# Where the moving operands of the first layer's products start: 32 bytes further into tiles that all start at multiples of 64 bytes

## The chip, the cores and the metric

The kernel runs on one core of one Trainium2 chip. The metric is the device time of one execution in microseconds; it is given as the median of several runs of the same program, and one further execution was taken with the hardware profiler.

## What is computed

Linear attention with an RMS norm per head, then a two-layer network with a GELU between its layers. The reference, cut to what matters:

```python
# q, k, v: (8, 8, 576, 64); g_norm: (64,); w_in: (512, 2048); w_out: (2048, 512)
kv = np.einsum('bhsd,bhse->bhde', k, v)
out = np.einsum('bhsd,bhde->bhse', q, kv)
rms = np.sqrt(np.mean(out * out, axis=-1, keepdims=True) + 1e-06)
out = out / rms * g_norm
x = out.transpose(0, 2, 1, 3).reshape(4608, 512)
h = x @ w_in
g = 0.5 * h * (1.0 + erf(h / sqrt(2)))
return g @ w_out
```

## The kernel before, in words

The 4608 tokens are cut into nine chunks of 512. Every operand of the two big layers is held as two float32r parts, a high and a low one, and a product takes three matmuls: high by high, low by high, high by low. Weights and activations stand in a pool named `const`, mostly in tiles of 128 partitions by 4096 bytes (`w_in0` to `w_in15`, `w_out0` to `w_out15`, `x0` to `x5`), which are used again for other things once their first content has been read.

Chunks 0 and 1 run the first layer plainly (`layer1`, L508 to L524): per block of 128 hidden units twelve matmuls of 512 columns, weights stationary, activations moving. While chunk 1 runs, the weights are summed and differenced into the seven operands of Strassen's scheme in Winograd's form and written to memory (`combine`, `high_sums`, `low_sums`, `product_out`).

Chunks 2 to 8 run the first layer by that scheme (`layer1_pair`, L412 to L450). Two hidden blocks form a pair j. It has seven products, and each is six matmuls (L427): the stationary operand is a 128 by 128 piece of one of four ring tiles, the moving one is 256 columns of one of seven pieces of the chunk's activations:

```python
    def product(k, out, first=False):
        n = ((at.c - PLAIN) * NF // 2 + j) * NPR + k
        w, x = ring[n // 2][:, n % 2 * DM:(n % 2 + 1) * DM], at.x[k]
        for kb in range(2):
            hi, lo = (w[:, m * HALF + kb * P:m * HALF + (kb + 1) * P] for m in range(2))
            for i, (y, z) in enumerate(((hi, 0), (lo, 0), (hi, 1))):
                nc.tensor.matmul(out=out, lhsT=y, rhs=x[:, z, kb], ...)
```

The ring tiles (`w_in0` to `w_in3`) are loaded again from memory as soon as their two products are done (`load_products`, L407 to L410). The seven pieces of a chunk stand in `x2`, `x3`, `w_in5` to `w_in9` for even chunks and in `x0`, `x1`, `x4`, `x5`, `w_in10` to `w_in12` for odd ones (`piece_tile`, L343 to L346). ScalarE writes a piece's high half (`high_block`, L317), GpSimd or VectorE its low half (`low_block`, L323), while the chunk before runs. Between the products VectorE adds their results in PSUM (L419, L437).

The second layer (`layer2`, L541 to L549) takes 24 matmuls of 512 columns per pair (L546): the GELU's results are stationary, the rows of `w_out` move. A chunk's eight pairs follow one another (L934 to L947): seven products, then the second layer of the pair before, with the next chunk's projections (`project`, L196 to L209, 64 to 512 columns of `qh` and `ql`, or of `w_in4`, moving against `kv_h` and `kv_l`) put between in the pairs 0 to 2.

The order on every engine is the order of the program (a manual schedule). The tensor engine's weight loads (PEld) run beside its matmuls (PE).

The program also has a tile `warm` of zeros (L78), on which 28 dummy matmuls run in the first 19 us (`keep_warm`, L596).

Of the kernel before, what the change touches and what calls it, by code (L numbers as in the profile page):

```python
# [8 lines left out]
F32 = mybir.dt.float32  # L9
F32R = mybir.dt.float32r  # L10
I32 = mybir.dt.int32
# [5 lines left out]
P = 128  # L17
EPS = 1e-6
CH = 512
# [3 lines left out]
HALF = CH // 2  # L23
# [12 lines left out]
def linear_attn_rms_gelu_ffn(  # L36
# [18 lines left out]
    NT, DM = out.shape  # L55
    B, NP = kv_main.shape[:2]
# [4 lines left out]
    NF = w_in.shape[0]  # L61
# [4 lines left out]
    const = ctx.enter_context(tc.tile_pool(name="const", bufs=1))  # L66
# [8 lines left out]
    kv_l = [const.tile([P, NP, P], F32R, name=f"kv_l{s}") for s in range(2)]  # L75
    ident = const.tile([P, P], F32, name="ident")
    fold = const.tile([P, P], F32, name="fold")
    warm = const.tile([P, P], F32, name="warm")  # L78
    half_g = const.tile([P, 1], F32, name="half_g")
    heads = const.tile([P, 2], F32, name="heads")  # L80


    kv_in, late = {}, {}

    def late_tile(name):

        if name not in late:
            late[name] = const.tile([P, 2 * DM], I32, name=name).bitcast(F32)
        return late[name]

    def load_main(b, p):
# [16 lines left out]
    def load_kv(b, p):  # L108

        early = b == 0 or (b == 1 and p > 1)  # L110
        if early:
            main = late_tile(f"w_out{NF - 1 - p if b == 0 else NF - 3 - p}")
        else:
            main = work.tile([P, 2 * DM], I32, name="kv_main", bufs=2).bitcast(F32)
        nc.sync.dma_start(out=main, in_=kv_main[b, p])
        main = main.rearrange("p (a n) -> p a n", a=2)[:KROWS]
        if b == 0:
            tails = late_tile(f"w_in{NF - 1}")[:TAIL].rearrange("p (a n) -> p a n", a=NP)
            if p == 0:
                nc.sync.dma_start(out=tails, in_=kv_tail[0])  # L120
            tail = tails[:, p]
        else:
            if early:
                tail = late_tile(f"w_in{NF - 5}")[:, (p - 2) * 2 * P:(p - 1) * 2 * P]
            else:
                tail = work.tile([P, 2 * P], I32, name="kv_tail", bufs=2).bitcast(F32)
            tail = tail[:TAIL]
            nc.sync.dma_start(out=tail, in_=kv_tail[b, :, p])
        tail = tail.rearrange("p (a n) -> p a n", a=2)
        parts = [main[:, :, j * P:(j + 1) * P] for j in range(NJ)] + [tail]  # L130
        kv_in[b, p] = [(t[:, 0], t[:, 1]) for t in parts]
# [29 lines left out]
    class Attn:  # L161
# [119 lines left out]
            self.low_x(p, eng)  # L281

        def high_x(self, p):
            x = const.tile([P, 2, CH], F32R, name=f"x{(NP * self.c + p) % 6}")
            nc.scalar.copy(out=x[:, 0], in_=self.o[p])
            self.x[p] = x

# [29 lines left out]
        def high_block(self, n):  # L317

            x = piece_tile(self.c, n)
            nc.scalar.copy(out=x[:, 0], in_=self.block(OPERANDS[n]))  # L320
            self.x[n] = x
# [13 lines left out]
    kept = {}  # L335

    def reused(i, dtype=F32):

        if i not in kept:
            kept[i] = const.tile([P, 2 * DM], dtype, name=f"w_in{i}")  # L340
        return kept[i]

    def piece_tile(c, n):  # L343
        k = (["x2", "x3"] + [f"w_in{i}" for i in range(5, 10)],
             ["x0", "x1", "x4", "x5"] + [f"w_in{i}" for i in range(10, 13)])[c % 2][n]
        return const.tile([P, 2, 2, HALF], F32R, name=k)  # L346

    products = [dram.tile([P, 2 * DM], F32, name=f"products{t}") for t in range(NT2)]

# [35 lines left out]
    def high_sums():  # L385

        for (j, second), s in stage.items():
            if j % 2:
                t = reused(second, F32R).rearrange("p (k a n) -> p k a n", k=2, a=2)
            else:  # L390
                t = const.tile([P, 2, 2, HALF], F32R, name=f"x{2 + second}")
            nc.scalar.copy(out=t[:, :, 0], in_=s)
            halved[j, second] = s, t
        stage.clear()
# [12 lines left out]
    def load_products(t):  # L407
        if t < (NCH - PLAIN) * NT2:
            ring[t] = reused(t % RING, F32R)
            nc.sync.dma_start(out=ring[t].bitcast(F32), in_=products[t % NT2])  # L410

    def layer1_pair(at, j, between):  # L412


        a, b = (ps_h.tile([P, CH], F32, name="ps_h") for _ in range(2))
        left, right = slice(0, HALF), slice(HALF, CH)
        u = reused(15).rearrange("p (a n) -> p a n", n=HALF)
        p1, u2, v, u3 = (u[:, i] for i in range(4))
        add = lambda out, x, y: nc.vector.tensor_tensor(out=out, in0=x, in1=y, op=ALU.add)  # L419
# [38 lines left out]
    raw, parts = {}, {}  # L458

    def load_w(n):  # L460
        kind, i = weights[n]
        src = w_in[i] if kind == "in" else w_out[i * P:(i + 1) * P, :]
        raw[n] = const.tile([P, 2 * DM], I32, name=f"w_{kind}{i}")
        nc.sync.dma_start(out=raw[n], in_=src.bitcast(I32))

    zs, ws = {}, {}
# [27 lines left out]

    def high_w(n):
        kind, i = weights[n]
        t = const.tile([P, 2 * DM], F32R, name=f"w_{kind}{i}")
        parts[kind, i] = t
        nc.scalar.copy(out=t[:, HI], in_=ws[n].bitcast(F32))

# [59 lines left out]

    attn = [Attn(c) for c in range(NCH)]
    first, second = attn[:2]
    nc.vector.memset(warm, 0.0)
    nc.scalar.activation(out=heads, in_=warm[:, :2], func=AF.Gelu)
    mask, g_row = late_tile(f"w_in{NF - 6}")[:, :P], late_tile(f"w_in{NF - 6}")[:1, P:2 * P]
# [11 lines left out]
    for h in range(2):  # L577
        nc.scalar.dma_start(out=g_row[:, h * D:(h + 1) * D], in_=g_norm.unsqueeze(0))
    load_w(0)
    for p in range(2):  # L580
        load_kv(1, p)
    for n in (1, 2, 3):
        load_w(n)
    for p in (2, 3):
        load_kv(1, p)
    load_w(4)
    second.load(0)
    for n in range(5, 9):
# [47 lines left out]
    n = 2 * NB  # L636
# [45 lines left out]
    for p in (2, 3):  # L682
        bcs[p] = ps_acc.tile([P, DM], F32, name=f"acc{p}")
        for t in range(NG):
            for h, r in enumerate((slice(0, D), slice(D, 2 * D))):
                k = n + 2 * ((p - 2) * NG + t) + h
# [82 lines left out]
    def sum_weights(i, n, gelu_rest):  # L769

        high_sums()
        for k in range(n):
            if k:
                high_sums()
            combine(*halves.pop(0))
            if not k:
                gelu_rest()
            low_sums()
        if not n:
            gelu_rest()  # L780
            low_sums()
# [22 lines left out]
    def convert(i, gelu_rest, between):  # L804

        count = 3 if i in (2, 4, 6, 8) else 2 if i < 11 else i in (11, 12, 14)
        now = [order.pop(0) for _ in range(count)]
        for k, n in enumerate(now or [None]):  # L810
            if last:
                high_w(last[0])
                if last[0] + 2 < len(weights):
                    top_w(last[0] + 2)
            if not i and not k:
                gelu_rest()
                low_w(last.pop())
            if n is not None:
                bits_w(n)
            if i and not k:  # L820
                gelu_rest()
            if last:
                low_w(last.pop())
            if n is not None:
                last.append(n)
            if not k:
                between()
# [7 lines left out]
    for s in range(PLAIN * NF):  # L835
        c, i = divmod(s, NF)
# [7 lines left out]
        if c == 0:  # L844
# [4 lines left out]
            def between():  # L849
                if i == 0:  # L850
                    for p in (2, 3):
                        attn[0].low_x(p, nc.vector)
                if i in (9, 10):
                    high_w(i - 9)
                    low_w(i - 9)
                if i == 1:
                    split_kv(1, range(NP))
                    nc.scalar.copy(out=kv_h[0], in_=kv_f)
                    nc.vector.tensor_tensor(
                        out=kv_l[0], in0=kv_f, in1=kv_h[0].bitcast(F32), op=ALU.subtract  # L860
                    )
                spread_work(c, i)
# [9 lines left out]
        else:  # L872
# [3 lines left out]
            n = 0 if not 1 <= i <= 11 else 2 if i in (1, 3, 5, 7, 11) else 1  # L876
# [116 lines left out]
```

## Time and profile before

| what | value |
|---|---|
| median of 3 runs | 837.55 us (836.57 to 837.58) |
| the profiled execution's own time | 836.58 us |
| its span, first to last instruction | 834.8 us |
| granted TensorE clock, mean | 1.000 of full speed |
| PE busy, share of the span | 99% |
| PEld busy, share of the span | 88% |
| VectorE busy, ScalarE busy | 59%, 38% |
| chain that ended last: L546 | 47% |
| chain that ended last: L427 | 34% |

How to read it: the page first gives each engine's busy time, then the chain of work that ended last, which is followed back from the last instruction, each time to what released it. Matmuls are pipelined, so the duration of one (here 283 ns for 256 columns) is not what it costs: in a stream the cost of one is the time from its start to the start of the next, called the pitch below. It is read from a timeline, as the time between two rows' starts divided by the matmuls between them. A weight load (LDWEIGHTS) has a duration of its own and runs beside the matmul before.

### The profile page before, as it was taken

To read this page: it belongs to the slowest core of one execution; us is meant where nothing else is said; L and a number is where in the kernel's file an instruction comes from. 1 tells how busy PE (TensorE), PEld (TensorE's weight loads), DVE (VectorE), ACT (ScalarE), POOL (GpSimd) and SP (SyncE) were. 2 spreads that over 40 slices of the span, in tenths; PEclk is the share of its full clock that TensorE was granted. 3 is DMA by queue.
4 is the path that set the end of the run, shared out by engine and by line. 5 is a ranking of instruction groups with operands and counts; after the bars stand their busy time and mean duration, and the time that the engine had idled before them with its cause. 6 is when DMAs were issued, how large, how long until landed. Compare 5 with 4: busy or idle time off the path is not lost.

```text
span 834.8 us, 13786 instructions
## 1 busy us (share of the span) xinstructions
PE 829.1 (99%) x5380; PEld 734.7 (88%) x5380; DVE 495.3 (59%) x980; ACT 314.2 (38%) x580; POOL 65.2 (8%) x67
## 2 busy tenths in 40 slices
PE   8999999999999999999999999999999999999998
PEld 7688888888999999999999999999999989999997
DVE  3999838687546744674457545673467446744442
ACT  2788444434531334233423253233323332322221
POOL 1000021011010101010001010010101000100000
PEclk9999999999999999999999999999999999999999
DMA  9981337776684568456955587456455655556551
GB/s 350 406 328 51 114 123 258 255 247 239 242 313 131 175 237 302 165 177 202 325 172 174 203 275 263 148 181 231 172 170 174 214 202 177 177 177 227 177 177 50
DMA packets 61460, 174.96 MB, mean 210 GB/s; under 512 B 6484, under 2 KB 15188, under 8 KB 61396
## 3 DMA queue, kind: packets, MB, share of 16 engines
q1 hardware_dynamic: 61392, 174.09, 59.8%
q8 instruction: 42, 0.69, 0.3%
q14 instruction: 22, 0.18, 0.1%
q10 hardware_dynamic: 4, 0.00, 0.0%
HBM read 149.95 MB, written 24.12 MB: 209 GB/s over the span
## 4 chain that ended last, share of the span: by engine, by line
PE 98%; DMA 1%; ACT 0%; issue 0%
PE acc L546 47%; PE ps_h L427 34%; PE ps_h L520 10%; PE ps_a L205 3%; PE ps_a L145 2%; DMA w_out<-kv_main 1%; PE ps_h L512 1%; PE acc L687 0%; PE acc L630 0%; PE ps_h L641 0%; PE ps_a L235 0%; PE ps_h L598 0%; ACT z L557 0%; PE ps_h L665 0%
## 5 line engine op out<-in xcount | busy, mean ns | idle before, releaser
L546 PE MATMUL acc<-w_out,gh 128*128 128x512 f32 x704 | 218.4, 392 | 0.0
L427 PE MATMUL ps_h<-w_in,w_in 128*128 128x256 f32 x1392 | 176.2, 283 | 0.0
L427 PEld LDWEIGHTS ps_h<-w_in,w_in 128*128 128x128 f32 x1392 | 171.1, 192 | 0.0
L546 PE MATMUL acc<-w_out,w_in 128*128 128x512 f32 x672 | 159.7, 392 | 0.0
L546 PEld LDWEIGHTS acc<-w_out,gh 128*128 128x128 f32 x704 | 130.1, 188 | 25.5
L546 PEld LDWEIGHTS acc<-w_out,w_in 128*128 128x128 f32 x672 | 124.1, 188 | 24.7
L546 PE MATMUL acc<-w_out,gl 128*128 128x512 f32 x352 | 137.2, 390 | 0.0
L532 ACT ACTIVATE gh<-ps_h 128x512 fp32r<-128x512 f32 x88 | 52.5, 597 | 212.6 <-DVE ps_h L419 155.3
L427 PEld LDWEIGHTS ps_h<-x,w_in 128*128 128x128 f32 x960 | 122.6, 191 | 4.4
L427 PE MATMUL ps_h<-x,w_in 128*128 128x256 f32 x960 | 123.9, 283 | 0.0
L532 ACT ACTIVATE w_in<-ps_h 128x512 fp32r<-128x512 f32 x56 | 33.5, 598 | 184.8 <-DVE ps_h L419 184.8
L437 DVE COPY w_in<-ps_h 128x256 f32<-128x256 f32 x56 | 23.8, 425 | 133.2 <-PE ps_h L427 133.2
L419 DVE TENSOR_TENSOR ps_h<-ps_h,w_in 128x256 f32<-128x256 f32 x168 | 72.7, 433 | 48.0 <-PE ps_h L427 43.6
L419 DVE TENSOR_TENSOR w_in<-ps_h,w_in 128x256 f32<-128x256 f32 x168 | 71.4, 425 | 49.1 <-PE ps_h L427 47.2
L520 PE MATMUL ps_h<-x,w_in 128*128 128x512 f32 x360 | 86.8, 390 | 0.0
L538 DVE TENSOR_TENSOR gl<-ps_h,gh 128x512 fp32r<-128x512 f32 x88 | 60.5, 687 | 42.7 <-ACT ps_h L533 38.2
L533 ACT ACTIVATE ps_h<-ps_h 128x512 f32<-128x512 f32 x144 | 85.4, 593 | 0.0
L520 PEld LDWEIGHTS ps_h<-x,w_in 128*128 128x128 f32 x360 | 67.5, 188 | 13.9 <-POOL x L290 0.2
L546 PEld LDWEIGHTS acc<-w_out,gl 128*128 128x128 f32 x352 | 66.1, 188 | 14.1
L538 DVE TENSOR_TENSOR w_in<-ps_h,w_in 128x512 fp32r<-128x512 f32 x56 | 38.5, 687 | 17.0 <-ACT ps_h L533 17.0
L193 POOL TENSOR_TENSOR ql<-q,qh 128x512 fp32r<-128x512 f32 x16 | 21.3, 1328 | 211.0 <-ACT qh L192 116.0
L325 POOL TENSOR_TENSOR w_in<-o,w_in 128x512 fp32r<-128x512 f32 x13 | 16.8, 1311 | 212.3 <-ACT w_in L320 212.3
(135 smaller groups left out, 635.5 us busy)
## 6 DMA issues: line engine op xcount, KB each, us to landing
w_in<-products SPq DMA_DIRECT2D x196, 512.0 KB, 4.7
products<-w_in SPq DMA_DIRECT2D x40, 256.0 KB, 3.2
kv_main<-kv_main SPq DMA_DIRECT2D x18, 512.0 KB, 6.7
w_in<-w_in SPq DMA_DIRECT2D x16, 512.0 KB, 10.2
w_out<-w_out SPq DMA_DIRECT2D x16, 512.0 KB, 10.2
q<-qT SPq DMA_DIRECT2D x15, 512.0 KB, 6.3
out<-w SPq DMA_DIRECT2D x18, 256.0 KB, 2.1
out<-z SPq DMA_DIRECT2D x18, 256.0 KB, 2.2
```

What stands on the lines that cost most here:

```text
L145: nc.tensor.matmul(out=ps[r, n * D:(n + 1) * D], lhsT=k[:, r], rhs=v[:, r], start=(j == 0), stop=(j == NJ),)
L193: eng.tensor_tensor(out=ql, in0=q, in1=qh.bitcast(F32), op=ALU.subtract)
L205: nc.tensor.matmul(out=ps[:, a:e], lhsT=w, rhs=x[:, a:e], start=(m == 0), stop=(m == 2))
L325: eng.tensor_tensor(out=x[:, 1], in0=self.block(OPERANDS[n]), in1=x[:, 0].bitcast(F32), op=ALU.subtract,)
L419: add = lambda out, x, y: nc.vector.tensor_tensor(out=out, in0=x, in1=y, op=ALU.add)
L427: nc.tensor.matmul(out=out, lhsT=y, rhs=x[:, z, kb], start=first and kb + i == 0, stop=kb == 1 and i == 2, skip_group_check=True,)
L437: nc.vector.tensor_copy(out=p1, in_=a[:, left])
L520: nc.tensor.matmul(out=h, lhsT=parts["in", i][:, w][:, p * P:(p + 1) * P], rhs=at.x[p][:, x], start=(m + p == 0), stop=(m == 2 and p == NP ...
L532: nc.scalar.activation(out=gh, in_=h, func=AF.Gelu)
L533: nc.scalar.activation(out=h, in_=h, func=AF.Gelu)
L538: nc.vector.tensor_tensor(out=gl, in0=h, in1=gh.bitcast(F32), op=ALU.subtract)
L546: nc.tensor.matmul(out=ps, lhsT=x[:, ts], rhs=parts["out", i][:, w], start=(i == 0 and m == 0), stop=(i == NF - 1 and m == 2),)
```

## The change

A new helper, `block_tile`, allocates the 4096-byte tiles. Those that ever hold a piece of the activations (`x0` to `x5`, `w_in5` to `w_in12`) get 64 bytes more, so that each tile still starts at a multiple of 64 bytes, and `piece_tile` returns a view that starts 8 elements, 32 bytes, into its tile. All other users of these tiles take the view that starts at 0. To make room the tile `warm` goes; its zeros now stand in columns 512 to 639 of `w_in10`, beside `mask` and `g_row`.

```diff
@@ -75,17 +75,25 @@
-    warm = const.tile([P, P], F32, name="warm")
     half_g = const.tile([P, 1], F32, name="half_g")
     heads = const.tile([P, 2], F32, name="heads")
+    SHIFT = 8
+    ROOM = {f"x{i}" for i in range(6)} | {f"w_in{i}" for i in range(5, 13)}
+
+    def block_tile(name, dtype, shift=0):
+        t = const.tile([P, 2 * DM + (2 * SHIFT if name in ROOM else 0)], dtype, name=name)
+        return t[:, shift:shift + 2 * DM]
...
-            late[name] = const.tile([P, 2 * DM], I32, name=name).bitcast(F32)
+            late[name] = block_tile(name, I32).bitcast(F32)
...
-            x = const.tile([P, 2, CH], F32R, name=f"x{(NP * self.c + p) % 6}")
+            x = block_tile(f"x{(NP * self.c + p) % 6}", F32R).rearrange("p (a n) -> p a n", a=2)
...
-            kept[i] = const.tile([P, 2 * DM], dtype, name=f"w_in{i}")
+            kept[i] = block_tile(f"w_in{i}", dtype)
...
     def piece_tile(c, n):
         k = (["x2", "x3"] + [f"w_in{i}" for i in range(5, 10)],
              ["x0", "x1", "x4", "x5"] + [f"w_in{i}" for i in range(10, 13)])[c % 2][n]
-        return const.tile([P, 2, 2, HALF], F32R, name=k)
+        return block_tile(k, F32R, SHIFT).rearrange("p (a b n) -> p a b n", a=2, b=2)
...
-                t = const.tile([P, 2, 2, HALF], F32R, name=f"x{2 + second}")
+                t = block_tile(f"x{2 + second}", F32R).rearrange("p (a b n) -> p a b n", a=2, b=2)
...
-        raw[n] = const.tile([P, 2 * DM], I32, name=f"w_{kind}{i}")
+        raw[n] = block_tile(f"w_{kind}{i}", I32)
...
-        t = const.tile([P, 2 * DM], F32R, name=f"w_{kind}{i}")
+        t = block_tile(f"w_{kind}{i}", F32R)
...
+    warm = late_tile(f"w_in{NF - 6}")[:, DM:DM + P]
     nc.vector.memset(warm, 0.0)
```

No engine's instructions change their order, number, shape or type. What changes is where operands stand, and one set of waits, on SP's queue, at the load of `w_in10`. On SP before (the numbers behind the names are buffer numbers):

```order
L464 DMA w_in9_188<-w_in 128x1024 [waits DMAHW6_49]
L464 DMA w_out8_190<-w_out 128x1024 [waits DMAHW7_49]
L464 DMA w_in10_192<-w_in 128x1024 [waits DMAHW0_49,DVE_49,Pool_49]
L464 DMA w_out9_194<-w_out 128x1024 [waits DMAHW1_49]
L464 DMA w_in11_196<-w_in 128x1024 [waits DMAHW2_49,DVE_49,PE_49]
```

and with the change:

```order
L472 DMA w_in9_187<-w_in 128x1024 [waits DMAHW6_49]
L472 DMA w_out8_189<-w_out 128x1024 [waits DMAHW7_49]
L472 DMA w_in10_191<-w_in 128x1024 [waits DVE_49,PE_49,DMAHW0_49,Activation_49,Pool_49]
L472 DMA w_out9_193<-w_out 128x1024 [waits DMAHW1_49]
L472 DMA w_in11_195<-w_in 128x1024 [waits DMAHW2_49,DVE_49,PE_49]
```

The load of `w_in10` now waits for PE and ScalarE too, which read the zeros in that tile.

The addresses, as the two built programs have them. Before, every tile in question starts at a multiple of 64 bytes, and the 4096-byte tiles follow one another without a gap. Take of each matmul the start of its moving operand, less the start of the stationary operand that is loaded while it runs (the next matmul's), modulo 128 bytes:

| line, columns | before | with the change |
|---|---|---|
| L427, 256 | 0 in 2328, 64 in 24 | 32 in 1166, 96 in 1186 |
| L205, 256 | 0 in 4, 64 in 20 | 0 in 2, 64 in 22 |
| L520, 512 | 0 in 356, 64 in 4 | 0 in 166, 64 in 194 |
| L546, 512 | 0 in 1715, 64 in 12 | 0 in 995, 64 in 732 |

(Lines by their numbers before the change.)

## Rows read from the trace of the kernel before

**Rows 1.** The page: busy time by engine, and the granted clock in 40 slices.

```profile
PE 829.1 (99%) x5380; PEld 734.7 (88%) x5380; DVE 495.3 (59%) x980; ACT 314.2 (38%) x580; POOL 65.2 (8%) x67
...
PEclk9999999999999999999999999999999999999999
```

**Rows 2.** The page: the chain that ended last, by line.

```profile
PE acc L546 47%; PE ps_h L427 34%; PE ps_h L520 10%; PE ps_a L205 3%; PE ps_a L145 2%; DMA w_out<-kv_main 1%; PE ps_h L512 1%; PE acc L687 0%; PE acc L630 0%; PE ps_h L641 0%; PE ps_a L235 0%; PE ps_h L598 0%; ACT z L557 0%; PE ps_h L665 0%
```

**Rows 3.** The page: L427's matmuls by operands (count, busy, mean ns, idle before).

```profile
L427 PE MATMUL ps_h<-w_in,w_in 128*128 128x256 f32 x1392 | 176.2, 283 | 0.0
...
L427 PE MATMUL ps_h<-x,w_in 128*128 128x256 f32 x960 | 123.9, 283 | 0.0
```

**Rows 4.** Busy time in one pair of a late chunk, 529.70 to 540.20 us.

```profile
core 0: us, PE busy (x) PEld busy (x) DVE busy (x) ACT busy (x) POOL busy (x), PEclk, DMA share, GB/s
529.70:540.20 10.50, 10.50 (x69) 9.54 (x68) 7.60 (x14) 2.80 (x6) 0.00 (x0) 1.00 0.52 174
```

**Rows 5.** Timeline of PE in that pair (start us, us, what).

```profile
533.79 0.62 PE L546 MATMUL acc<-w_out,gh 128*128 128x512 f32 x2
...
534.47 0.62 PE L546 MATMUL acc<-w_out,gh 128*128 128x512 f32 x2
534.93 0.39 PE L546 MATMUL acc<-w_out,gl 128*128 128x512 f32 x1
535.15 3.04 PE L427 MATMUL ps_h<-x,w_in 128*128 128x256 f32 x24
538.03 2.32 PE L427 MATMUL ps_h<-w_in,w_in 128*128 128x256 f32 x18
540.19 0.40 PE L546 MATMUL acc<-w_out,w_in 128*128 128x512 f32 x1
```

**Rows 6.** Timeline of PE where L205 has 256 columns, behind L427, twice.

```profile
301.86 0.28 PE L205 MATMUL ps_a<-qh,kv_h 128*128 128x256 f32 x1
...
302.43 0.28 PE L205 MATMUL ps_a<-ql,kv_h 128*128 128x256 f32 x1
302.54 0.63 PE L546 MATMUL acc<-w_out,gh 128*128 128x512 f32 x2
...
313.04 0.28 PE L205 MATMUL ps_a<-w_in,kv_h 128*128 128x256 f32 x1
...
313.72 1.55 PE L546 MATMUL acc<-w_out,w_in 128*128 128x512 f32 x6
```

**Rows 7.** The same where it stands behind L546.

```profile
316.47 0.28 PE L205 MATMUL ps_a<-qh,kv_h 128*128 128x256 f32 x1
...
317.17 2.21 PE L546 MATMUL acc<-w_out,w_in 128*128 128x512 f32 x9
```

**Rows 8.** Timeline of PE where matmuls have two columns, so that weight loads set the pitch.

```profile
14.41 1.02 PE L641 MATMUL ps_h<-heads,ql 128*128 128x2 f32 x8
15.30 0.39 PE L665 MATMUL ps_h<-part,fold 128*128 128x32 f32 x2
```

**Rows 9.** Timeline of PE where L205 has 512 columns.

```profile
659.70 0.39 PE L205 MATMUL ps_a<-qh,kv_h 128*128 128x512 f32 x1
...
660.38 0.62 PE L546 MATMUL acc<-w_out,gh 128*128 128x512 f32 x2
```

**Rows 10.** Timeline of DVE between the products of that pair.

```profile
532.46 0.69 DVE L538 TENSOR_TENSOR w_in<-ps_h,w_in 128x512 fp32r<-128x512 f32 x1 [0.62 <-ACT ps_h L533]
...
536.79 0.43 DVE L437 COPY w_in<-ps_h 128x256 f32<-128x256 f32 x1 [0.81 <-PE ps_h L427]
537.25 0.42 DVE L419 TENSOR_TENSOR w_in<-ps_h,w_in 128x256 f32<-128x256 f32 x1
```

**Rows 11.** The ring's loads, L410: from issue to landing.

```profile
DMA to landing us min/median/max: 3.1/4.7/8.6
```

**Rows 12.** Timelines: the last dummy matmuls, and SP's load of `w_in10`.

```profile
18.35 0.71 PE L598 MATMUL ps_h<-warm 128*128 128x128 f32 x4
...
39.07 0.33 SPq L464 DMA_DIRECT2D w_in<-w_in  x1
```

## The prediction, as put on record

> **What bounds the kernel now.** [...] L427 runs 1392 + 960 = 2352 matmuls of 256 columns [rows 3].
>
> Then look at one pair of a late chunk in the table of busy times: 10.50 us long, PE busy for all of it, PEld for 9.54, VectorE for 7.60, ScalarE for 2.80, the DMA engines for about half [rows 4]. No other engine bounds such a pair.
>
> Last, the timeline of that pair, for the pitch, the time from one matmul's start to the next one's. L427 starts at 535.15, its second row at 538.03, L546 at 540.19 [rows 5]: 24 matmuls in 2.88 us, 18 in 2.16, so 120.0 ns each in both. In L546 three matmuls take 0.68 us (533.79 to 534.47), 227 ns each. The difference, 256 columns more, costs 107 ns, so one column costs 0.417 ns. 256 columns at that rate would be 106.7 ns; both kinds of matmul pay some 13 ns on top of it. That extra is what an address could change. Beside each matmul the next one's weights are loaded from the same memory. The floor that these loads set is seen where matmuls have two columns only: eight take 0.89 us (14.41 to 15.30), 111 ns each [rows 8].
>
> The row that decides is a line that the change doesn't touch. L205 also has matmuls of 256 columns with 128 stationary ones. Behind L427 six of them take 0.68 us (301.86 to 302.54, and 313.04 to 313.72), 113.3 ns each [rows 6], with the same shapes, type and clock as L427's 120.0. What differs is the address: there the moving operand lies an odd multiple of 64 bytes from the weights that are loaded meanwhile (but for a set's last matmul), in L427 a multiple of 128. Behind L546 such a set takes 0.70 us (316.47 to 317.17), 116.7 ns each [rows 7]. So the cost on top depends on how the two streams lie, and L427 sits in the dearest of the positions seen. It is no proof: the sets are six matmuls long, and another thing about that line could be the cause.
>
> **The change part by part.**
>
> *L427, the shifted operands.* The distance modulo 128 goes from 0 to 32 or 96 in all 2352. No row of before has a full-rate matmul at such a distance, so the price is bounded. From below: nothing can beat the weight loads' 111 ns [rows 8], a gain of at most 8.7 ns each, 2352 x 8.7 = 20.5 us. From above: 1024 bytes that start 32 bytes off reach into 17 blocks of 64 bytes where they filled 16. If such a block is read whole, a matmul pays 16 columns more, 16 x 0.417 = 6.7 ns, or 2352 x 6.7 = 15.7 us lost. I take the nearest rows, those of the same shape with operands out of step. Each of the 56 bursts (7 chunks, 8 pairs) stands behind matmuls of L546 or of a fold; I give its first six matmuls the 116.7 ns of the set behind L546 [rows 7], the other 36 the 113.3 [rows 6]. That is 56 x (6 x 3.3 + 36 x 6.7) ns = 56 x 261 ns = 14.6 us gained.
>
> *L546 and L520, moved along.* Because fourteen tiles grow by 64 bytes, 732 matmuls of L546 and 194 of L520 now stand at an odd multiple of 64 bytes, where almost none did. The only rows of 512 columns at such a distance are L205's: three in 0.68 us (659.70 to 660.38) [rows 9], as in L546 now [rows 5]. So I take nothing. The timeline rounds to 10 ns, which over three matmuls leaves 3 ns either way: 926 x 3 = 2.8 us for the range.
>
> *The zeros in `w_in10`.* The memset, the dummy matmuls and the activation are the same instructions. What is added is that SP's load of `w_in10` waits for them too. SP issues it at 39.07 us; the last dummy matmuls run from 18.35 for 0.71 us [rows 12]. The cover is 20 us, so the cost is nothing; without cover each us late would delay the loads queued behind it on SP.
>
> *What is late next.* A faster L427 shortens what hides beside it. VectorE's copy and addition behind product 1 end at 537.25 + 0.42 = 537.67, and product 4, which writes over what they read, starts at 538.03 [rows 5, 10]: 0.36 us to spare. Both ends move with L427, the copy's by 12 matmuls and product 4's by 24, so the margin shrinks by 12 x 6.7 = 0.08 us. The GELU's last reader of the accumulators ends at 532.46 + 0.69 = 533.15, two us before the next products [rows 5, 10]. A ring tile is loaded again one pair, some 10 us, before it is needed, and the slowest load landed in 8.6 us [rows 11]; a pair 0.26 us shorter leaves over one us. In the pairs with the next chunk's work VectorE's margin may be less; I allow 1 us in the range.
>
> *Sum.* The profiled execution took 836.6 us around a span of 834.8: 836.6 - 14.6 = 822.0. The median of the runs shown is 837.55, 1.0 higher, so against it the change gives **823.0 us**, -1.7%. A measurement of this kernel can tell about 0.2% from no change, 1.7 us.
>
> **The rivals.**
>
> *Half a gain.* The bursts stay in the position of the set behind L546, 116.7 ns throughout [rows 7]. For it: every burst comes from such a place, and 32 is halfway to the 64 for which rows exist. Against: L205's other sets show that 113.3 holds over six matmuls [rows 6]. 2352 x 3.3 = 7.8 us less: 829.8 us.
>
> *No change.* The 13 ns belong to every change of weights and not to the address. For it: L546, L520 and L427 pay nearly the same with many tiles and offsets, and L205's 512 columns, at an odd distance, pay it too [rows 5, 9]. Against: the sets at 113.3 and 116.7 ns [rows 6, 7]. All 2352 pitches stay at 120.0: 837.5 us. [...]
>
> *Slower: the 17th block.* If the moving operand is read in aligned blocks of 64 bytes, with nothing carried from one matmul to the next, each L427 matmul reads one block more while the conflict stays as it is: 126.7 ns. Its place is every matmul of L427, its price 2352 x 6.7 = 15.7 us, so 853.2 us. It decides as soon as the extra block costs more than the better position saves, at a pitch over 120 ns. For it: PE has no idle time to absorb it [rows 4], and all operands of full-rate matmuls start at multiples of 64 bytes now, so no row excludes it. Against: if the position costs nothing any more, 106.7 + 6.7 = 113.4 ns would still beat 120.
>
> **How the numbers follow.** The forecast has 0.42, half a gain 0.20, no change 0.17, slower 0.21. The row at 113.3 is the nearest in shape, which is why it leads; that no row has a distance of 32 or 96 is why it has less than half. Faster by over 0.2% is 0.42 + 0.20 = 0.62, within 0.2% 0.17, slower 0.21. The range of the forecast alone is 817 (the floor of the weight loads: 837.5 - 20.5) to 827 (823 with 2.8 for L546 and L520 and 1 for VectorE). To hold 8 in 10 it reaches over half a gain and no change, 837.5, and some of the small losses: 817 to 840.
>
> **What would show it.** In the profile after, the rows of L427 in a late pair should lie 42 x 113.3 to 116.7 ns apart, 4.8 us instead of 5.04, and the pair should last some 10.24 us with PE busy throughout; L546 should keep 0.68 us per three. The load of `w_in10` should still be issued near 39 us. The prediction is wrong if L427's pitch is 120 (no effect of the address) or above (the 17th block), if L546's pitch moves by more than 3 ns, or if the pitch falls and PE shows idle time before L427 that eats the gain.

## The result and the profile after

The change makes the kernel slower by half a per cent: median 841.3 us against 837.83 in the same session (12 runs each), a ratio of 1.0045 with a 95% interval of 1.0033 to 1.0056. In a second session it came out at 1.0036 (1.0022 to 1.0049). The forecast was 823.0 us, with a range of 817 to 840.

The page after gives the lines that answer to [rows 3], and those of the second layer (L554, before L546) and of the plain first layer (L528, before L520):

```profile
L554 PE MATMUL acc<-w_out,gh 128*128 128x512 f32 x704 | 220.5, 394 | 0.0
L435 PE MATMUL ps_h<-w_in,w_in 128*128 128x256 f32 x1392 | 173.7, 281 | 0.0
...
L554 PE MATMUL acc<-w_out,w_in 128*128 128x512 f32 x672 | 161.6, 394 | 0.0
...
L554 PE MATMUL acc<-w_out,gl 128*128 128x512 f32 x352 | 138.3, 393 | 0.0
...
L435 PE MATMUL ps_h<-x,w_in 128*128 128x256 f32 x960 | 122.4, 280 | 0.0
...
L528 PE MATMUL ps_h<-x,w_in 128*128 128x512 f32 x360 | 88.4, 394 | 0.0
```

The page of the kernel before has for the two lines of 512 columns:

```profile
L546 PE MATMUL acc<-w_out,gh 128*128 128x512 f32 x704 | 218.4, 392 | 0.0
...
L546 PE MATMUL acc<-w_out,w_in 128*128 128x512 f32 x672 | 159.7, 392 | 0.0
L546 PE MATMUL acc<-w_out,gl 128*128 128x512 f32 x352 | 137.2, 390 | 0.0
...
L520 PE MATMUL ps_h<-x,w_in 128*128 128x512 f32 x360 | 86.8, 390 | 0.0
```

The number behind the bar is a group's busy time. L427 (after: L435) falls from 176.2 + 123.9 = 300.1 us to 173.7 + 122.4 = 296.1, by 4.0. The second layer rises from 218.4 + 159.7 + 137.2 = 515.3 to 220.5 + 161.6 + 138.3 = 520.4, by 5.1, and L520 from 86.8 to 88.4, by 1.6.

Busy times of groups that overlap, with each matmul's whole duration in them (393 to 394 ns on the page after for the second layer, where one starts every 232 ns on the mean), give the direction but not the cost. What a line costs the engine is the sum of the times from each of its matmuls' starts to the next start in the trace. By these starts L427 falls from 281.85 to 277.84 us, by 4.0, the second layer rises from 395.12 to 400.68, by 5.6, and L520 from 82.28 to 83.90, by 1.6. Together that is 3.2 us more, of the 3.5 by which the span grew, from 834.8 to 838.3.

The timeline of PE after, over two late pairs, shows both prices:

```profile
532.94 0.63 PE L554 MATMUL acc<-w_out,gh 128*128 128x512 f32 x2
...
533.64 0.63 PE L554 MATMUL acc<-w_out,gh 128*128 128x512 f32 x2
...
537.13 0.61 PE L554 MATMUL acc<-w_out,gh 128*128 128x512 f32 x2
...
537.81 0.61 PE L554 MATMUL acc<-w_out,gh 128*128 128x512 f32 x2
...
538.49 3.00 PE L435 MATMUL ps_h<-x,w_in 128*128 128x256 f32 x24
541.33 2.27 PE L435 MATMUL ps_h<-w_in,w_in 128*128 128x256 f32 x18
543.44 5.73 PE L554 MATMUL acc<-w_out,w_in 128*128 128x512 f32 x24
549.01 2.98 PE L435 MATMUL ps_h<-x,w_in 128*128 128x256 f32 x24
```

The products: 42 matmuls from 538.49 to 543.44, 4.95 us or 117.9 ns each, where [rows 5] had 120.0. The second layer: its first pair uses `w_out6`, whose rows lie 192 bytes (modulo 256) from the weights loaded meanwhile, and then `w_out7`, at 0. Three matmuls take 0.70 us at the start (532.94 to 533.64, 233 ns each) and 0.68 us at the end (537.13 to 537.81, 227 ns, as before); the first three at 0 still take 0.70 (535.75 to 536.45). The next pair, with `w_out8` and `w_out9` at 128, takes 5.57 us for its 24 (543.44 to 549.01), 232 ns each.

So the shifted products did become cheaper, by 4.0 us where 14.6 were forecast, and the second layer, which the change does not name, became dearer by more. That the 64 bytes of growth did it, and what the 32 bytes did, the experiments had to show.

### The profile page after: what moved, and what is told of

Same layout as the page of the kernel before. It is cut to its first block, busy times and chain, and to the rows that moved or that the text cites. A ratio compares the mean times of both kernels' runs of the same rounds, so it can differ in the third digit from the quotient of the medians.

```text
span 838.3 us, 13787 instructions
## 1 busy us (share of the span) xinstructions
PE 832.3 (99%) x5380; PEld 730.6 (87%) x5380; DVE 495.0 (59%) x980; ACT 314.8 (38%) x580; POOL 65.0 (8%) x67
## 4 chain that ended last, share of the span: by engine, by line
PE 98%; DMA 1%; SPq 0%; ACT 0%; issue 0%; DVE 0%
PE acc L554 48%; PE ps_h L435 33%; PE ps_h L528 10%; PE ps_a L213 3%; PE ps_a L153 2%; PE ps_h L520 1%; DMA w_out<-kv_main 1%; PE acc L639 0%; PE acc L696 0%; PE ps_h L650 0%; PE ps_a L243 0%; PE ps_h L607 0%; ACT z L565 0%; SPq L181 0%; SPq L128 0%
## 5 line engine op out<-in xcount | busy, mean ns | idle before, releaser
L554 PE MATMUL acc<-w_out,gh 128*128 128x512 f32 x704 | 220.5, 394 | 0.0
L435 PE MATMUL ps_h<-w_in,w_in 128*128 128x256 f32 x1392 | 173.7, 281 | 0.0
L435 PEld LDWEIGHTS ps_h<-w_in,w_in 128*128 128x128 f32 x1392 | 168.4, 188 | 0.0
L554 PE MATMUL acc<-w_out,w_in 128*128 128x512 f32 x672 | 161.6, 394 | 0.0
L554 PEld LDWEIGHTS acc<-w_out,gh 128*128 128x128 f32 x704 | 130.0, 188 | 27.8
L554 PEld LDWEIGHTS acc<-w_out,w_in 128*128 128x128 f32 x672 | 124.1, 188 | 26.4
L554 PE MATMUL acc<-w_out,gl 128*128 128x512 f32 x352 | 138.3, 393 | 0.0
L435 PEld LDWEIGHTS ps_h<-x,w_in 128*128 128x128 f32 x960 | 121.2, 188 | 4.8
L435 PE MATMUL ps_h<-x,w_in 128*128 128x256 f32 x960 | 122.4, 280 | 0.0
L427 DVE TENSOR_TENSOR ps_h<-ps_h,w_in 128x256 f32<-128x256 f32 x168 | 72.6, 432 | 46.9 <-PE ps_h L435 42.3
L427 DVE TENSOR_TENSOR w_in<-ps_h,w_in 128x256 f32<-128x256 f32 x168 | 71.4, 425 | 47.5 <-PE ps_h L435 45.6
L528 PE MATMUL ps_h<-x,w_in 128*128 128x512 f32 x360 | 88.4, 394 | 0.0
L546 DVE TENSOR_TENSOR gl<-ps_h,gh 128x512 fp32r<-128x512 f32 x88 | 60.5, 687 | 45.4 <-ACT ps_h L541 40.8
L528 PEld LDWEIGHTS ps_h<-x,w_in 128*128 128x128 f32 x360 | 67.4, 188 | 15.3
L554 PEld LDWEIGHTS acc<-w_out,gl 128*128 128x128 f32 x352 | 66.1, 188 | 15.4
L546 DVE TENSOR_TENSOR w_in<-ps_h,w_in 128x512 fp32r<-128x512 f32 x56 | 38.4, 686 | 17.1 <-ACT ps_h L541 17.1
```

The source lines that it names most:

```text
L435: nc.tensor.matmul(out=out, lhsT=y, rhs=x[:, z, kb], start=first and kb + i == 0, stop=kb == 1 and i == 2, skip_group_check=True,)
L528: nc.tensor.matmul(out=h, lhsT=parts["in", i][:, w][:, p * P:(p + 1) * P], rhs=at.x[p][:, x], start=(m + p == 0), stop=(m == 2 and p == NP ...
L546: nc.vector.tensor_tensor(out=gl, in0=h, in1=gh.bitcast(F32), op=ALU.subtract)
L554: nc.tensor.matmul(out=ps, lhsT=x[:, ts], rhs=parts["out", i][:, w], start=(i == 0 and m == 0), stop=(i == NF - 1 and m == 2),)
```

## The experiments

Below, "the distance" is the start of a matmul's moving operand less that of the stationary operand loaded while it runs, modulo 256 bytes, in the built program. Modulo 256 the kernel before has 0 nearly everywhere in L427, L520 and L546. Line numbers shift with each edit: L428, L433 and L435 are L427, and L547, L552 and L554 are L546. All experiments compute all that the kernel computes.

**The growth without the shift** (`room_only`, and once more as `room_again` beside the change itself, `after_again`).

```diff
-        return block_tile(k, F32R, SHIFT).rearrange("p (a b n) -> p a b n", a=2, b=2)
+        return block_tile(k, F32R).rearrange("p (a b n) -> p a b n", a=2, b=2)
```

> The change without its shift: the fourteen tiles have their 64 bytes more and the zeros stand in w_in10, but the pieces start at 0 of their tiles. Theory (two effects of opposite sign: the 32 bytes make the first layer's products cheaper, the 64 bytes more per tile move the second layer's and L520's operands off a distance of 0 modulo 256 and make those dearer): the second layer stays as in the profile after, 24 matmuls in 5.48 to 5.60 us where before had 5.46, and L427 has its cost by its own mix of distances 0, 64, 128 and 192. If distances other than 0 are worth to L427 what they are after (118 ns), about 841 us; if only odd multiples of 32 help L427, 845 us (837.8 + 5.6 for the second layer + 1.6 for L520). Rival (the second layer is slow only because the shifted L427 hands over in another state): second layer back at 227 ns in all pairs, 837 us or less.

> The change itself once more, on the same chip as the next run, so that the two differ by the 32 bytes alone. Theory: 1.0045 of before, L427's 2352 matmuls in 277.8 us; about 1 us above the run without the shift.

> The change without its shift (the tiles' 64 bytes more stay). Theory (at 256 columns any distance but 0 helps, so that the 32 bytes add nothing to what the tiles' growth brought): within 1.5 us of the change, below it rather than above, about 840 us. Rival (the shift helps by itself): at least 2 us above the change.

Measured: 1.0033 of before (1.0017 to 1.0049) in the first session, 1.0031 (1.0019 to 1.0043) in the second, where the change itself had 1.0036 (1.0022 to 1.0049); the medians of that session are 839.65 us without the shift and 840.19 with it. The intervals overlap: the time cannot tell the change with its shift from the change without. The page of the second run without the shift can:

```profile
L554 PE MATMUL acc<-w_out,gh 128*128 128x512 f32 x704 | 220.7, 394 | 0.0
L435 PE MATMUL ps_h<-w_in,w_in 128*128 128x256 f32 x1392 | 172.9, 280 | 0.0
...
L554 PE MATMUL acc<-w_out,w_in 128*128 128x512 f32 x672 | 161.3, 394 | 0.0
...
L554 PE MATMUL acc<-w_out,gl 128*128 128x512 f32 x352 | 138.4, 393 | 0.0
...
L435 PE MATMUL ps_h<-x,w_in 128*128 128x256 f32 x960 | 122.3, 281 | 0.0
...
L528 PE MATMUL ps_h<-x,w_in 128*128 128x512 f32 x360 | 88.4, 394 | 0.0
```

The second layer stands at 220.7 + 161.3 + 138.4 = 520.4 us, as with the shift, and L528 at 88.4: the loss is the growth's, and the rival that the shifted L427 slows the second layer fell. L427 stands at 172.9 + 122.3 = 295.2 us, 0.9 below the change with its shift; from start to start it is 276.96 against 277.84 us. So the growth, which spread L427 over the distances 0, 64, 128 and 192, had brought all of the products' gain, and the 32 bytes on top took a little of it back.

**The zeros alone** (`zeros_moved`).

```diff
-    warm = const.tile([P, P], F32, name="warm")
...
+    warm = late_tile(f"w_in{NF - 6}")[:, DM:DM + P]
     nc.vector.memset(warm, 0.0)
```

> The kernel before with only the zeros of the dummy matmuls moved into w_in10 and the tile warm gone, so that all later tiles stand 512 bytes lower and no distance modulo 256 changes. Theory: nothing changes, 837.8 us within 0.2%, L427 at 120 ns, second layer at 227. Rival (the waits that this adds to SP's load of w_in10 are part of the loss): up to 3.5 us slower.

Measured: 837.41 us, a ratio of 1.0000 (0.9985 to 1.0015). The zeros and the waits that they add to SP cost nothing.

**Only the second layer moved** (`work_192`, `work_32`, `work_224`): the kernel before with 64, 224 or 32 bytes ahead of the pool that holds `gh` and `gl`.

```diff
     HI, LO = slice(0, DM), slice(DM, 2 * DM)
...
+    work.tile([P, 16], F32, name="pad")
     kv_in, late = {}, {}
```

> The kernel before with 64 bytes put ahead of the pool that holds gh, gl, qh and ql, and nothing else: for 997 matmuls of the second layer (those with gh and gl as weights) the distance goes from 0 to 192 modulo 256, for the 718 with w_in13 and w_in14 it stays 0, L427 stays at 0. Theory (the second layer lost because its operands left a distance of 0): the 997 at 233.4 ns, as pairs at 192 have in the profile after, 997 x 6.7 = 6.7 us more, 844 us; the 718 and L427 as before. Rival (it lost because w_out tiles at several distances follow one another, or because of what L427 hands over): all at 227 ns, 837.5 us.

> The same with 224 bytes, so that these 997 matmuls lie at a distance of 32. No run has 512 columns at an odd multiple of 32 yet. Theory: the price at 512 columns rises steadily with the distance (227 at 0, 230.6 at 64, 232.3 at 128, 233.4 at 192 after), so 227 to 230 ns, up to 3 us more: 837.5 to 841 us. Rival (a shift of half a block helps every matmul, as it helps at 256 columns): below 227 ns, 834 us or less.

> The same with 32 bytes: a distance of 224. Theory: between the 233.4 ns of 192 and the 227 of 0, up to 997 x 6.7 = 6.7 us more: 838 to 844 us. Rival (half a block helps): below 227 ns, under 836 us.

The pad also moves those matmuls of the other two lines whose next weights lie in that pool, 16 of L427 and 26 of L520.

Measured: 1.0075 of before (1.0057 to 1.0092) at 192, 1.0081 (1.0054 to 1.0107) at 32, 1.0070 (1.0049 to 1.0090, two runs) at 224. The timeline of PE with the distance at 192 has both cases next to each other, `gh` and `gl` as weights (192) and then `w_in13` or `w_in14` (0):

```profile
534.53 0.63 PE L547 MATMUL acc<-w_out,gh 128*128 128x512 f32 x2
...
540.13 3.02 PE L428 MATMUL ps_h<-x,w_in 128*128 128x256 f32 x24
542.99 2.32 PE L428 MATMUL ps_h<-w_in,w_in 128*128 128x256 f32 x18
545.15 5.63 PE L547 MATMUL acc<-w_out,w_in 128*128 128x512 f32 x24
550.62 3.04 PE L428 MATMUL ps_h<-x,w_in 128*128 128x256 f32 x24
```

24 matmuls take 5.60 us at 192 (534.53 to 540.13) and 5.47 at 0 (545.15 to 550.62), 233 against 228 ns, while L427 between them keeps 5.02 us. At a distance of 32 it is the same 5.60 us:

```profile
533.19 0.62 PE L547 MATMUL acc<-w_out,gh 128*128 128x512 f32 x2
...
538.79 3.03 PE L428 MATMUL ps_h<-x,w_in 128*128 128x256 f32 x24
```

So the distance by itself made matmuls of 512 columns dearer, 233 ns against 228, without any change to L427. It is the place of one operand against the other that counted, and not either one's own: here `gh` and `gl` moved and the rows of `w_out` stayed, while in the pair of the profile after `gh` and `gl` kept one place modulo 256 and `w_out6` cost 233 ns where `w_out7` came to cost 227. The expectation that the price rises steadily from 0 fell: 32 and 224 cost as much as 192. Of the distances that runs have, only 0 is cheap at 512 columns; 64, which 158 matmuls have in the profile after, takes 231 ns there on the mean.

**Only L427 moved** (`ring_32`, `ring_64`, `ring_96`, `ring_192`, `ring_224`): the kernel before with the four ring tiles 256 bytes longer and read so many bytes into the tile that L427 alone gets one distance (2296 of its 2352 matmuls); the zeros stand in `w_in10` to make room. The weights move here, and the pieces still start at multiples of 64 bytes. The last matmul of the second layer before each burst, 56 in all, gets the new distance too.

```diff
+    SHIFT = 56
+    ROOM = {f"w_in{i}" for i in range(RING)}
+    def block_tile(name, dtype, shift=0):
+        t = const.tile([P, 2 * DM + (64 if name in ROOM else 0)], dtype, name=name)
+        return t[:, shift:shift + 2 * DM]
...
-            kept[i] = const.tile([P, 2 * DM], dtype, name=f"w_in{i}")
+            kept[i] = block_tile(f"w_in{i}", dtype, SHIFT if i < RING else 0)
```

> The shift without the growth of fourteen tiles: the kernel before, with the ring tiles w_in0 to w_in3 256 bytes longer and read 224 bytes into the tile, so that L427's moving operands lie 32 modulo 256 from the weights, and every other distance stays as before. Theory: L427 at the 117.3 ns that the trace after has at a distance of 32, 2352 x 2.7 = 6.3 us less than before; second layer and L520 at 227 ns: 831.5 us. Rival (what the change lost comes from the shifted operand itself, for instance a 17th block of 64 bytes): no gain, 838 us or more.

> The same with the ring tiles read 192 bytes in: a distance of 64 in L427, the one at which L205 took 113.3 ns behind L427 and 116.7 behind the second layer. Theory: L427 between these two, 2352 x 3.3 to 6.7 = 7.8 to 15.7 us less: 822 to 830 us. Rival (L205's rows owe their price to something else than the address): L427 at 120 ns, 837.8 us; or only odd multiples of 32 bytes help: 837.8 us as well.

> As ring_32 and ring_64, with the ring tiles read 64 bytes in: a distance of 192 in L427 alone, which had the cheapest mean of the four in the run without the shift, 116.7 ns. Theory (any distance but 0 helps at 256 columns, by 2 to 3 ns, and the odd multiple of 32 is nothing special): 116 to 118 ns, 2352 x 2 to 4 = 5 to 9 us less than before, 828 to 832 us. Rival (the 32 bytes matter): 119 ns or more, 835 us or more.

> The ring tiles read 32 bytes in, a distance of 224 in L427 alone. Theory: 116 to 118.5 ns as at 32, 64 and 192: 829 to 834 us. Rival (some distance frees L427 wholly, down to the weight loads' 111 to 113 ns): 822 us or less.

> The same at a distance of 96, the dearest of the four in the profile after (119.0 ns among mixed distances). Theory: 116 to 119 ns when it is the only distance, 829 to 835 us. Rival as for the run before: 822 us or less.

Measured, with L427's price from one late burst of 42 (its first row's start to the start of the matmul behind it):

| distance in L427 | burst of 42, us | ns each | median, us | ratio to before |
|---|---|---|---|---|
| 0 (before) | 5.04 | 120.0 | 837.2 to 837.8 | 1 |
| 32 | 4.90 | 116.7 | 831.4 | 0.9922 (0.9895 to 0.9949) |
| 64 | 4.94 | 117.6 | 832.35 | 0.9940 (0.9920 to 0.9960) |
| 96 | 5.03 | 119.8 | 837.21 | 1.0005 (0.9990 to 1.0019) |
| 192 | 4.94 | 117.6 | 831.69 | 0.9938 (0.9922 to 0.9953) |
| 224 | 4.98 | 118.6 | 835.01 | 0.9973 (0.9961 to 0.9985) |

The timeline of PE at 32, and then at 96:

```profile
533.12 2.96 PE L433 MATMUL ps_h<-x,w_in 128*128 128x256 f32 x24
535.92 2.26 PE L433 MATMUL ps_h<-w_in,w_in 128*128 128x256 f32 x18
538.02 5.62 PE L552 MATMUL acc<-w_out,w_in 128*128 128x512 f32 x24
543.48 2.96 PE L433 MATMUL ps_h<-x,w_in 128*128 128x256 f32 x24
```

```profile
536.69 3.04 PE L433 MATMUL ps_h<-x,w_in 128*128 128x256 f32 x24
539.57 2.31 PE L433 MATMUL ps_h<-w_in,w_in 128*128 128x256 f32 x18
541.72 5.64 PE L552 MATMUL acc<-w_out,w_in 128*128 128x512 f32 x24
```

At 32 the burst lasts from 533.12 to 538.02, 4.90 us, and the second layer behind it 5.46 us (538.02 to 543.48), which is its price before. Here a distance of 32 does what the change's shift was meant to do, because almost nothing else moves: `ring_32` is faster than both kernels, by 0.8% against before. From start to start its L427 takes 274.50 us, 7.4 less than before. The theory that any distance but 0 helps at 256 columns fell at 96, which is worth nothing. Distances of 128 and 160 were not tried alone; among mixed distances their means are 118.3 ns (`room_only`) and 118.1 (the change).

The run at 64 also shows how far L205's cheap sets can be carried over. Its timeline has the set of [rows 6] again, with the same instructions at the same distance:

```profile
300.89 0.28 PE L211 MATMUL ps_a<-qh,kv_h 128*128 128x256 f32 x1
...
301.60 0.63 PE L552 MATMUL acc<-w_out,gh 128*128 128x512 f32 x2
```

Six matmuls now take 0.71 us, 118 ns each, where they took 0.68 in [rows 6]. What changed is what runs ahead of them: L427 at 117.6 ns where it had been at 120. The other runs of this group agree: behind L427 at 96, which costs 119.8 ns, the set takes 0.68 us again (303.25 to 303.93), and behind 32, 192 and 224 it takes 0.70 (302.10 to 302.80, 300.81 to 301.51, 303.41 to 304.11). So in these runs the price went with what ran before as well as with the distance, and 42 in a row at a distance of 64 settled at 117.6, not at 113.3. Why the matmuls before matter is not shown.

## Why the prediction was wrong, point by point

*What bounds the kernel* held: PE stayed busy for 99% of the span, no wait appeared, and nearly all the difference, 3.2 of 3.5 us, lies in the time that a matmul holds the engine. One reading in it was empty: that both kinds of matmul pay the same 13 ns on top follows from drawing a line through two points. What an address changes is not a common extra; off a distance of 0 the runs show up to 3 ns less at 256 columns and 4 to 6 ns more at 512.

*L427, the shifted operands* had the right sign and the wrong size. It took "the nearest rows", L205's sets, and gave 36 of 42 matmuls 113.3 ns: 14.6 us. It measured 4.0. The rows were of the right shape but only six matmuls long, and in the runs that moved L427 alone their 113.3 ns stood only where L427 stayed at 120; where L427 became cheaper, as it was meant to, they took 116.7 to 118. The rival "half a gain", 116.7 ns and 7.8 us, is close to what a distance of 32 is worth alone: L427 took 7.4 us less, and the median fell from 837.2 to 831.4, 5.8 us. In the change it was worth less still, because 64 bytes more per tile spread the products over 32, 96, 160 and 224, of which alone 96 is worth nothing and 224 less than half of 32.

*L546 and L520, moved along* is the step that failed: "So I take nothing", with 2.8 us for the range. They cost 5.6 + 1.6 = 7.2 us, and the second layer's pitch moved by 5 to 6 ns at 128 and 192, which the prediction had named as a sign of being wrong (more than 3). Two things were wrong in it. It priced them by three matmuls of L205, 0.68 us [rows 9], two at a distance of 64 and the last at 0; three or six matmuls behind another line are no price, as the run at 64 showed, and in the profile after whole pairs or half pairs at 128 and 192 take 232 to 234 ns each. And it counted distances modulo 128, by which 355 matmuls that the change moved by 128 bytes (281 of L546, 74 of L520) seemed to stay where they were. The period is longer: at 128 the second layer costs 232 ns, at 0 it costs 227. Had both layers been counted modulo 256, the change would have read as what it is, a move of both lines off 0; what that costs, no row of before could have said. The kernel before has nearly all of its matmuls at 0 because its tiles, from the first one of 4096 bytes on, are multiples of 256 bytes long; it had that for nothing, and lost it by 64 bytes.

Both errors were needed. With 4.0 us gained and nothing lost it would have been faster; with 7.2 lost and 14.6 gained as well.

*The zeros* and *what is late next* held: moving the zeros alone measured 1.0000, SP issued the load of `w_in10` at 38.29 us, and PE was busy throughout a late pair after as before (10.50 of the 10.50 us from 532.94 to 543.44).

*The rivals.* The slower one named a wrong mechanism: by the author's estimate a 17th block at L427 would have put its pitch at 126.7 ns, and it fell to 117.9; that operands are read in blocks of 64 bytes is shown by no run. The loss came from a line that the forecast had set to zero. "No change", that the address has no part in the price, fell with every run in which a distance moved but the one at 96: 120.0 against 116.7 ns at 256 columns and 228 against 233 at 512 differ by addresses alone.

## What to carry to other kernels

Before moving one operand by a few bytes, list for every costly line where its moving operand stands from the weights loaded beside it, and hold all other distances fixed: here moving the weights of the line with 256 columns alone gained 0.8%, while the padding, which moved all lines at once, gained 4.9 us on that line and lost 7.1 on the two with 512. Six matmuls in a row are no price (113 or 118 ns here at one distance); use stretches of dozens, or a run that puts the line in question at the distance in question.

## What was not expected of the hardware

In these runs the distance between the two operands, modulo 256 bytes, changed the price of a float32r matmul by up to 3%, in opposite directions at two widths: at 512 columns 0 was the cheapest of those measured (228 against 232 to 233 ns at 32, 128, 192 and 224), at 256 columns 0 was the dearest, together with 96 (120.0 and 119.8), and 32 the cheapest (116.7). In `ring_64` distances that differ by 256 cost the same: half of the matmuls lie 64 and half 320 bytes off, counted modulo 512, and both halves have a mean of 117.8 ns. A short set's price also went with what ran before it: 113 ns behind L427 at 120, and 117 to 118 ns behind a cheaper L427, at one and the same distance. Why the sign turns is open; no run here separates the matmul's own stream from the weight load's, nor the next weights from those in use, which share their place modulo 256 within a burst. The weight loads' own pace, 111 ns [rows 8], was held through a burst at no distance; the lowest was 116.7.
